# Block records by ScalarE, fewer weight transfers and a later subtraction in an attention and expert kernel

## The chip, the cores and the metric

The kernel runs on one core of a Trainium2 chip. A time is that of one execution on the device, in microseconds; lower is better. Before the change three timed runs gave 525.13, 525.26 and 527.0 us. The profiled execution, from which every duration below is read, took 523.72 us; its profile spans 521.8 of them.

## The reference

Sigmoid attention over 8 batches, 12 heads, 448 positions of width 64, and behind it a mixture of experts on the 3584 rows of 768 that it gives. A token goes to one expert of eight, and only where its skip score is above zero; all others keep the attention's output.

```python
attn = 1.0 / (1.0 + np.exp(-scores))
attn_out = np.matmul(attn, v)
...
do_compute = x @ w_skip > 0
e_idx = np.argmax(xc @ w_gate, axis=1)
gate_w = probs[np.arange(len(xc)), e_idx]
for e in range(E):
    h = np.maximum(xc[mask] @ w1[e], 0.0)
    y[mask] = gate_w[mask, None] * (h @ w2[e])
out[do_compute] = xc + y
```

The weights w1 are 768 x 1024 and w2 1024 x 768 for each expert, all in float32.

## The kernel before

The attention fills the first 280 us: a static list of steps, one for each batch and pair of heads. While it runs, each token's gate value and row number go as a record of 16 numbers into a list in device memory, `lst`, one stretch for each expert. At its end the kernel plans the rest on VectorE (lines 897 to 1086): how many blocks of tokens each expert gets, in which order, and at which row of `lst` each block begins. The two blocks of the first expert run before the loop, with their matmuls written out between the planning steps.

Then comes a loop (line 1565), one arm for each block, and each arm is one of four kinds. A **full** arm (`block(i, False)`) takes 128 tokens with weights that are split into a high and a low part (wh, wl), three matmuls for each product. A **split** arm (`block(i, True)`) does the same and also splits the next expert's raw weights: ScalarE casts raw to wh (`hi1`, `hi2`), VectorE subtracts to wl (`lo1`, `lo2`), and GpSimd subtracts the last two of w2. A **half** (64 tokens) or **few** arm (32) takes the rest of an expert straight from its raw weights, and behind its matmuls SyncE issues the weights of the next expert (`load_w1`, `load_w2`). In the profiled execution the order is split, half, full, half, full, few, full, few, full, few, split, few, full, few.

Inside an arm the order on each engine is written out by hand. For the prediction these steps matter. `look_ahead` and `entry` load registers from the small table `slots`. `take_rec` copies the loaded record `rn` into `recs[:, 2]`; `advance` shifts the records by one block at the arm's end. `fetch`, on GpSimd, reads row numbers from `rn`, gathers the tokens `xn` of the block after next from `out`, and then gathers the next record into `rn`; TensorE turns `xn` round in the next arm (`turn_x`, into pxt). `put`, on GpSimd, copies the row numbers `rid` to `rp[0]` and adds the block's output to `out` by an indirect store; its small operations named jk read a few numbers of the output and so test that it is there. `shift` moves the list of row numbers `rix` by one block. The block before the loop gets its two first records and tokens by GpSimd gathers (`gather_rec`, `gather`), and eight first weight transfers go out on SyncE and ScalarE.

## Time and profile before

| | before |
|---|---|
| median of three timed runs | 525.26 us |
| profiled execution | 523.72 us |
| its span | 521.8 us |
| TensorE busy | 506.6 us |
| VectorE busy | 298.0 us |
| ScalarE busy | 278.8 us |
| GpSimd busy | 266.6 us |

In the profile PE is TensorE and PEld its loading of weights, DVE is VectorE, ACT ScalarE, POOL GpSimd and SP SyncE; a q behind a name is the engine's instruction queue. A row of the timeline gives the start, the duration, the engine, the line of the program, the operation, the tile written and those read, and in brackets how long the engine had been idle and what ended that.

### The profile page before, as it was taken

Reading aid. Unit: us, or ns where it says so; the run is one execution under the profiler, and the core shown is the slowest. Engines: PE = TensorE matmul, PEld = TensorE weight load, DVE = VectorE, ACT = ScalarE, POOL = GpSimd, SP = SyncE. Lnnn points to the kernel's source line nnn. Section 1 sums busy time; section 2 is a strip of 40 time slices with the busy share of each in tenths; the row PEclk is TensorE's granted clock in tenths of the full one; section 3 lists DMA queues with packets and bytes.
Section 4 is the critical chain, followed back from the end, with each engine's and each line's share of the span. In section 5 each row is a group of like instructions: output and inputs, shape, how many; then the busy total and the mean of one; then the engine's idle time right before and its main releaser. Section 6 shows DMA issues by size and latency. Waiting matters only on the chain.

```text
span 521.8 us, 15390 instructions
## 1 busy us (share of the span) xinstructions
PE 506.6 (97%) x5033; PEld 341.5 (65%) x5034; DVE 298.0 (57%) x721; ACT 278.8 (53%) x481; POOL 266.6 (51%) x418
## 2 busy tenths in 40 slices
PE   8999999999999999999999999999999999999991
PEld 6875555545555446555455989948669797978790
DVE  4556856658668678587684952872223323249532
ACT  5776776767767667677674211942122323267221
POOL 4523553443557775766674332373333545456654
PEclk9999999999999999999999999999999999999996
DMA  8998887897989989999955017859393969696932
GB/s 210 214 248 187 174 178 160 171 179 174 202 187 239 234 193 206 206 217 219 197 117 119 11 42 241 336 169 360 98 355 139 329 234 346 237 348 214 361 121 47
DMA packets 140288, 107.21 MB, mean 205 GB/s; under 512 B 97099, under 2 KB 112731, under 8 KB 140240
## 3 DMA queue, kind: packets, MB, share of 16 engines
q1 hardware_dynamic: 133456, 96.09, 69.8%
q0 software_dynamic: 4576, 8.65, 6.9%
q10 hardware_dynamic: 2208, 1.83, 1.1%
q8 instruction: 30, 0.49, 0.4%
q14 instruction: 18, 0.15, 0.1%
HBM read 98.49 MB, written 17.56 MB: 222 GB/s over the span
## 4 chain that ended last, share of the span: by engine, by line
PE 95%; ACT 1%; DVE 1%; POOL 1%; issue 1%; DMA 1%; ACTq 0%; POOLq 0%; DVEq 0%
PE s L212 25%; PE pa L240 24%; PE py L544 11%; PE ph L516 11%; PE b_ph L516 3%; PE b_py L544 3%; PE py L1416 3%; PE ph L1416 3%; PE py L1485 2%; PE ph L1485 2%; PE pxt L492 2%; PE pl L280 2%; PE pht L530 1%; PE pg L297 1%; DMA kq_first<-in_q_dram 1%
## 5 line engine op out<-in xcount | busy, mean ns | idle before, releaser
L232 ACT ACTIVATE at<-s,bias 128x896 f32<-128x896 f32 (+1 forms) x191 | 173.8, 913 | 79.5 <-PE s L212 70.5
L212 PE MATMUL s<-x 64*64 64x448 f32 (+1 forms) x1528 | 170.2, 496 | 0.7 <-DVE x L194 0.7
L240 PE MATMUL pa<-at,v 64*64 64x448 f32 (+1 forms) x1536 | 168.5, 490 | 0.0
L176 POOL COPY kq<-kq 32x896 f32<-32x896 f32 (+1 forms) x96 | 87.7, 913 | 92.3 <-DMA kq<-in_q_dram 56.3
L212 PEld LDWEIGHTS s<-x 64*64 64x64 f32 x1528 | 83.9, 191 | 49.1 <-issue 25.2
L240 PEld LDWEIGHTS pa<-at,v 64*64 64x64 f32 x1536 | 65.6, 133 | 55.0 <-issue 45.7
L194 DVE STREAM_TRANSPOSE x<-kq 128x448 f32<-128x448 f32 x94 | 81.0, 936 | 4.4 <-PE pa L240 4.4
L250 DVE TENSOR_TENSOR xt<-xt,pa 128x448 f32<-128x448 f32 x48 | 29.8, 620 | 52.6 <-ACT xt L673 52.6
L414 POOL DMA_INDIRECT lst<-rec,idx x32 | 31.7, 990 | 17.8 <-DVE xt L250 5.7
L486 POOL TENSOR_TENSOR wl<-wr,wh 128x384 fp32r<-128x384 f32 (+1 forms) x28 | 31.2, 1124 | 12.8 <-DVE wh L485 8.3
L255 DVE STREAM_TRANSPOSE y<-xt 128x448 f32<-128x448 f32 x48 | 31.0, 645 | 5.8 <-DMA out_dram<-y 4.4
L574 POOL DMA_INDIRECT out_dram<-ys,rp x15 | 23.5, 1570 | 16.6 <-issue 8.4
L525 ACT ACTIVATE hs<-ph 128x512 f32<-128x512 f32 x14 | 8.4, 597 | 42.8 <-PE ph L516 34.8
L544 PE MATMUL py<-wh,hh 128*128 128x384 f32 x112 | 29.9, 348 | 0.0
L544 PE MATMUL py<-wh,hl 128*128 128x384 f32 x112 | 28.9, 339 | 0.5 <-DVE hl L536 0.5
L544 PE MATMUL py<-wl,hh 128*128 128x384 f32 x112 | 28.7, 337 | 0.0
L502 DVE TENSOR_TENSOR xl<-pxt,xh 128x384 fp32r<-128x384 f32 x30 | 15.3, 552 | 21.3 <-ACT xf L1097 20.8
L516 PE MATMUL ph<-wl,xh 128*128 128x512 f32 x84 | 26.6, 403 | 0.0
L536 DVE TENSOR_TENSOR hl<-pht,hh 128x512 fp32r<-128x512 f32 x14 | 9.7, 690 | 29.6 <-ACT hh L535 28.2
L673 ACT ACTIVATE xt<-pa 128x448 f32<-128x448 f32 x48 | 25.7, 535 | 0.8 <-PE pa L240 0.8
L516 PE MATMUL ph<-wh,xh 128*128 128x512 f32 x84 | 25.7, 403 | 0.0
L516 PE MATMUL ph<-wh,xl 128*128 128x512 f32 x84 | 24.5, 396 | 0.0
(279 smaller groups left out, 686.8 us busy)
## 6 DMA issues: line engine op xcount, KB each, us to landing
raw<-in_moe_w_dram SPq DMA_DIRECT2D x62, 768.0 KB
v<-in_v_dram SPq DMA_DIRECT2D x48, 256.0 KB
out_dram<-y SPq DMA_DIRECT2D x192, 56.0 KB
kq<-in_k_dram SPq DMA_DIRECT2D x46, 224.0 KB
kq<-in_q_dram SPq DMA_DIRECT2D x46, 224.0 KB
wr<-in_moe_w_dram SPq DMA_DIRECT2D x12, 256.0 KB
wr<-in_moe_w_dram SPq DMA_DIRECT2D x16, 192.0 KB
lst<-fill SPq DMA_DIRECT2D x4, 464.0 KB
```

What stands on the lines that cost most here:

```text
L176: nc.gpsimd.tensor_copy(a[BT:, :, :, :BT], a[:BT, :, :, BT:])
L194: nc.vector.transpose(xs[:, n].rearrange("p (r j) -> p j r", j=NJ), t.rearrange("p (j d) -> p j d", d=D)[:, :, :BT],)
L212: nc.tensor.matmul(sc[m * D : (m + 1) * D, j, : qs.stop - qs.start], xs[r, 0, first::NR7], xs[r, 1, qs], start=True, stop=True,)
L232: nc.scalar.activation(at[:, :, :n], sc[:, :, :n], AF.Sigmoid, bias=bias, scale=SCALE)
L240: nc.tensor.matmul(pa[j * D : (j + 1) * D, r, qs], vt[rs, j, r + c if c < 3 else 3 * (1 - r), :], at[rs, j, : qs.stop - qs.start], start=( ...
L250: nc.vector.tensor_tensor(x, x, pa[:, 1, :S], op=ALU.add)
L255: nc.vector.transpose(y, xts[b][:, hp, :])
L414: put = nc.gpsimd.indirect_dma_start(out=lst[:, :], out_offset=bass.IndirectOffsetOnAxis(ap=idx[:, c : c + 1], axis=0), in_=rec[:, c, :], ...
L486: nc.gpsimd.tensor_tensor(lo, r, hi, op=ALU.subtract)
L516: nc.tensor.matmul(ph[h], a[:, j * P : (j + 1) * P], w[j][h], start=(n == 0), stop=(n == len(t) - 1),)
L544: last = nc.tensor.matmul(half_y(py, o), a[h][:, js], w[j][:, o * H2 : (o + 1) * H2], start=(j == 0 and n == 0), stop=(j == NK2 - 1 and n ...
L1416: nc.tensor.matmul(dst[g * SM : (g + 1) * SM, :n], a, w, start=(j == 0), stop=(j == most - 1), tile_position=(0, g * SM),)
```

## The change

The table of row numbers for every lane goes, and with it the matmul that spread it and the VectorE operations that made it. The plan's table `slots` gets a fourth line, the row of `lst` at which a block's record begins. A record is then 128 rows in one piece: the first three come by plain transfers on SyncE, and in the loop one comes on ScalarE (`next_rec`) in place of the gather on GpSimd. `shift` goes. The cast of the row numbers moves from `advance` to `take_rec` of the next arm. In a split arm GpSimd's two subtractions go behind its store. The raw weights w1 come in three transfers in place of four, and the last two first transfers of w2 move from ScalarE's queue to SyncE's, ahead of the others.

```diff
     V.tensor_scalar(m_p, rho, af, f_p, op0=ALU.is_equal, op1=ALU.mult)
-    V.tensor_scalar(row, m_f, f_rf, None, op0=ALU.mult)
-    V.scalar_tensor_tensor(row, m_a, f_ra, row, op0=ALU.mult, op1=ALU.add)
-    V.scalar_tensor_tensor(row, m_p, f_rp, row, op0=ALU.mult, op1=ALU.add)
     gemm1(1, range(3), xh0, xl0, ph)
-    nc.tensor.matmul(ptab[:, :NS], ones_f, row, start=True, stop=True)
-    HAS, NXT, TYP = range(3)
-    for n, (j, m) in enumerate(((2, m_a), (7, m_p), (12, m_f))):
+    ROW, HAS, NXT, TYP = range(4)
+    for n, (j, m) in enumerate(((1, m_a), (6, m_p), (11, m_f))):
         nc.tensor.matmul(
-            ptab[:3, NS : 2 * NS], gt[:NS, j : j + 3], m, start=(n == 0), stop=(n == 2)
-        )
-    V.tensor_scalar(rix, ptab[:, :NS], slot_q, None, op0=ALU.add)
-    slots = const.tile([3, NS], I32, name="slots")
-    V.tensor_scalar(slots, ptab[:3, NS : 2 * NS], 0.25, None, op0=ALU.add)
+            ptab[:4, :NS], gt[:NS, j : j + 4], m, start=(n == 0), stop=(n == 2)
+        )
+    slots = const.tile([4, NS], I32, name="slots")
+    V.tensor_scalar(slots, ptab[:4, :NS], 0.25, None, op0=ALU.add)
     def entry(j, col, engines, most):
         return nc.values_load(slots[j : j + 1, col], engines=engines, min_val=0, max_val=most)
...
                 AF.Copy,
             )
-    def ready_x():
+    def ready_x(pieces=3):
         for h in range(2):
             hi_x(h, pxt[h], xh)
         for h in range(2):
-            whole_x(h, [slice(j, j + 1) for j in range(3)])
+            whole_x(h, [slice(j, j + 3 // pieces) for j in range(0, 3, 3 // pieces)])
         for h in range(2):
             lo_x(h, pxt[h], xh, xl)
-    def gather_rec(dst, idx):
-        nc.gpsimd.indirect_dma_start(
-            out=dst,
-            out_offset=None,
-            in_=lst[:, :],
-            in_offset=bass.IndirectOffsetOnAxis(ap=idx, axis=0),
-            bounds_check=NE * CAP - 1,
-            oob_is_err=False,
-        )
+    def load_rec(dst, col, engines=SP, queue=nc.sync):
+        row = entry(ROW, col, engines, NE * CAP - P)
+        queue.dma_start(dst, lst[ds(row, P), :])
     for j in range(2):
-        gather_rec(recs[:, j, :], rix[:, j + 2 : j + 3])
-    gather_rec(rn, rix[:, 4:5])
+        load_rec(recs[:, j, :], slice(j + 2, j + 3))
+    load_rec(rn, slice(4, 5))
     gemm1(1, range(3, 9), xh0, xl0, ph)
     turn0(0)
     nc.vector.tensor_copy(rid[:, 0:1], recs[:, 0, 1:2])
...
 
-    w1s = iter([(h, g) for h in range(2) for g in range(2)])
-    raw1g = {}
+    parts1 = ((0, 0, 3), (0, 3, NK1), (1, 0, NK1))
+    raw1g = []
     raw2g = []
     def some1(n):
         for _ in range(n):
-            h, g = next(w1s)
-            raw1g[h, g] = mo.tile([P, 3, H1], F32, name=f"raw1_{h}_{g}")
+            h, a, z = parts1[len(raw1g)]
+            raw1g.append(mo.tile([P, z - a, H1], F32, name=f"raw1_{h}_{a}"))
     def some2(n):
         for _ in range(n):
...
     def next_expert(col):
         return entry(NXT, col, SP, NE - 1), entry(HAS, col, SP, 1)
-    def load_w1(g, h, nx):
+    def load_w1(n, nx):
+        h, a, z = parts1[n]
         return nc.sync.dma_start(
-            raw1g[h, g],
-            w1[ds(nx[0], 1), g * 3 * P : (g + 1) * 3 * P, h * H1 : (h + 1) * H1].rearrange(
+            raw1g[n],
+            w1[ds(nx[0], 1), a * P : z * P, h * H1 : (h + 1) * H1].rearrange(
                 "o (i p) f -> p (o i) f", p=P
             ),
             cond=nx[1],
         )
-    def load_w2(g, nx, queue=nc.sync):
-        queue.dma_start(
+    def load_w2(g, nx):
+        nc.sync.dma_start(
             raw2g[g],
             w2[ds(nx[0], 1), g * 2 * P : (g + 1) * 2 * P, :].rearrange(
                 "o (i p) f -> p (o i) f", p=P
...
         nc.values_load(first_i[0:1, 0:1], engines=SP, min_val=0, max_val=1),
     )
-    nx_act = (
-        nc.values_load(first_i[0:1, 1:2], engines=[ET.Activation], min_val=0, max_val=NE - 1),
-        nc.values_load(first_i[0:1, 0:1], engines=[ET.Activation], min_val=0, max_val=1),
-    )
-    for n in range(4):
-        load = load_w1(n % 2, n // 2, nx)
+    for n in range(3):
+        load = load_w1(n, nx)
         if n == 1:
             tc.add_manual_dep(
                 load.ins,
...
             )
         if n == 0:
             look_ahead(slice(2, 3))
-    for g in range(4):
-        load_w2(g, nx if g < 2 else nx_act, nc.sync if g < 2 else nc.scalar)
+            for g in range(2, 4):
+                load_w2(g, nx)
+    for g in range(2):
+        load_w2(g, nx)
     def fetch():
         pool.tensor_tensor(xn[:, 0:1], xn[:, 0:1], zf, op=ALU.add)
-        pool.tensor_tensor(jk, rn[:, 0:2], rn[:, 0:2], op=ALU.add)
         pool.tensor_copy(ri, rn[:, 1:2])
-        pool.tensor_tensor(rn[:, 0:1], rn[:, 0:1], zf, op=ALU.add)
-        pool.tensor_tensor(rx, rix[:, 5:6], zero, op=ALU.add)
         pool.tensor_tensor(rp[1], ri, zero, op=ALU.add)
         pool.tensor_tensor(rq, rp[1], zero, op=ALU.add)
         got = gather(xn, rp[1])
         tc.declare_no_dep(got.ins, group="put", across_iterations=True, reason="a token is in one block only")
         tc.add_to_no_dep_group("got", got.ins)
-        gather_rec(rn, rx)
-    def shift(eng):
-        for to, src in ((riv, rix[:, 6:NS]), (rix[:, 5 : NS - 1], riv)):
-            if eng is pool:
-                eng.tensor_tensor(to, src, zero.to_broadcast([P, NS - 6]), op=ALU.add)
-            else:
-                eng.tensor_copy(to, src)
+    def next_rec(i):
+        load_rec(rn, ds(i + 5, 1), [ET.Activation], nc.scalar)
     def put(n, last=None):
 
...
             nc.vector.tensor_copy(sv[:, j * n : (j + 1) * n], recs[:, 1 + j * n : 1 + (j + 1) * n, 0:2])
         for j in range(pieces):
             nc.vector.tensor_copy(recs[:, j * n : (j + 1) * n, 0:2], sv[:, j * n : (j + 1) * n])
+    def take_rec():
+        nc.vector.tensor_copy(recs[:, 2, 0:2], rn[:, 0:2])
         nc.vector.tensor_copy(rid[:, 0:1], recs[:, 0, 1:2])
-    def take_rec():
-        nc.vector.tensor_copy(recs[:, 2, 0:2], rn[:, 0:2])
     def weigh_sum(y, p, gate):
         nc.vector.tensor_scalar(y, p, gate, None, op0=ALU.mult)
...
         if last:
             for h in range(2):
                 whole_x(h, (slice(0, 3),))
-            shift(dve)
         else:
-            ready_x()
+            ready_x(1)
+        next_rec(i)
         for j in range(1, NK2):
             gemm2(j, hh, hl, py)
         if last:
...
                 lo2(j)
             for j in range(NK2 - 2, NK2):
                 dve.tensor_copy(wh2[j], raw2[j])
-                pool.tensor_tensor(wl2[j], raw2[j], wh2[j], op=ALU.subtract)
             for h in range(2):
                 lo_x(h, pxt[h], xh, xl)
-        else:
-            shift(dve)
         for o in range(2):
             rows = ys if last else yt
             weigh_sum(rows[:, o * H2 : (o + 1) * H2], half_y(py, o), recs[:, 0, 0:1])
         put(P, last)
         advance(1 if last else 2)
         if last:
-            for j in range(2, NK2 - 2):
-                lo2(j)
+            for j in range(2, NK2):
+                lo2(j, dve if j < NK2 - 2 else pool)
     def few(i):
 
...
                 nc.vector.scalar_tensor_tensor(
                     yt[:SM, s], p, recs[:SM, 0, 0:1], yt[:SM, s], op0=ALU.mult, op1=ALU.add
                 )
+        next_rec(i)
         put(SM)
         advance()
 
```

On GpSimd, at the end of a split arm, these stand before the change, from the gather of the next record to the jump back. In the names, raw_3 holds the raw weights, wh_6 and wl_6 the high and low part of one slice of w2, rp_4354 the row numbers of the block.

```order
L1115 DMA rn<-lst,rx 128x16
L1396 TENSOR_TENSOR wl_6_130<-raw_3_4371,wh_6_122 128x768
L1396 REGISTER_ALU
L1396 TENSOR_TENSOR wl_7_131<-raw_3_4371,wh_7_123 128x768
L1308 TENSOR_TENSOR rp_4354<-rid,zero 128x1
L1309 REGISTER_ALU
L1309 TENSOR_TENSOR rs<-rp_4354,zero 128x1
L1314 REGISTER_ALU
L1314 TENSOR_TENSOR jk<-ys 128x2
L574 DMA out_dram<-ys,rp_4354 3584x768
L1560 UNCONDITIONAL_BRANCH
```

The same place on GpSimd with the change (the names' numbers differ by build):

```order
L561 DMA xn<-out_dram,rp_4370 128x768
L1280 REGISTER_ALU
L1280 TENSOR_TENSOR rp_4369<-rid,zero 128x1
L1281 REGISTER_ALU
L1281 TENSOR_TENSOR rs<-rp_4369,zero 128x1
L1286 REGISTER_ALU
L1286 TENSOR_TENSOR jk<-ys 128x2
L571 DMA out_dram<-ys,rp_4369 3584x768
L1224 REGISTER_ALU
L1224 TENSOR_TENSOR wl_6_127<-raw_3_4383,wh_6_119 128x768
L1224 REGISTER_ALU
L1224 TENSOR_TENSOR wl_7_128<-raw_3_4383,wh_7_120 128x768
```

The gather of the record is gone, and the two subtractions stand behind the store, the last work of the arm.

On VectorE, in a split arm before the change, from the first high-low difference of the hidden values (hl) on; the cast of rid stands at the arm's end, behind the copies that advance the records:

```order
L536 TENSOR_TENSOR hl_4352<-pht,hh_4349 128x512
L1343 COPY recs<-rn 128x2
L1234 REGISTER_ALU
L1234 TENSOR_TENSOR wl_3_0_110<-raw_0_1_4348,wh_3_0_98 128x512
...
L1336 COPY sv<-recs 128x4
L1338 REGISTER_ALU
L1338 COPY recs<-sv 128x2x2
L1339 ISA
L1339 CAST rid<-recs 128x1
L1240 REGISTER_ALU
L1240 TENSOR_TENSOR wl_2_126<-raw_1_4368,wh_2_118 128x768
```

The same places on VectorE with the change:

```order
L533 TENSOR_TENSOR hl_4367<-pht,hh_4364 128x512
L1314 COPY recs<-rn 128x2
L1315 REGISTER_ALU
L1315 CAST rid<-recs 128x1
L1216 REGISTER_ALU
L1216 TENSOR_TENSOR wl_3_0_107<-raw_0_3_4363,wh_3_0_95 128x512
...
L1308 COPY sv<-recs 128x4
L1310 REGISTER_ALU
L1310 COPY recs<-sv 128x2x2
L1224 REGISTER_ALU
L1224 TENSOR_TENSOR wl_2_123<-raw_1_4380,wh_2_115 128x768
```

The cast has moved from the arm's end to the middle of the next arm, behind hl and the copy of the record; in a few or half arm `take_rec` is the first work of VectorE.

On SyncE, ahead of the loop, from the first loads of `slots`; before the change:

```order
L1089 TENSOR_LOAD slots
L1089 ISA x2
L1213 ISA
L1213 DMA raw_0_0_4347<-in_moe_w_dram 128x3x512
L1213 ISA
L1213 DMA raw_0_1_4348<-in_moe_w_dram 128x3x512
```

With the change:

```order
L1079 TENSOR_LOAD slots
L1079 ISA x2
L1105 ISA
L1105 DMA recs<-lst 128x16
L1079 TENSOR_LOAD slots
L1079 ISA x2
...
L1195 DMA raw_0_0_4362<-in_moe_w_dram 128x3x512
L1204 ISA
L1204 DMA raw_2_4382<-in_moe_w_dram 128x2x768
L1204 ISA
L1204 DMA raw_3_4383<-in_moe_w_dram 128x2x768
L1195 ISA
```

Three record transfers with their register loads now stand ahead of the first weights, and the transfers of raw_2 and raw_3 ahead of the second weight transfer.

## Rows read from the trace of the kernel before

**Rows 1.** The page: busy time of each engine with its share of the span and its instructions, and the shares of the chain that ended last, by engine.

```profile
PE 506.6 (97%) x5033; PEld 341.5 (65%) x5034; DVE 298.0 (57%) x721; ACT 278.8 (53%) x481; POOL 266.6 (51%) x418
...
PE 95%; ACT 1%; DVE 1%; POOL 1%; issue 1%; DMA 1%; ACTq 0%; POOLq 0%; DVEq 0%
```

**Rows 2.** The waits of TensorE's matmuls from 280 us to the end, two of three (the third, 0.2 us, lies at 281 us): who waited for whom; total us, times, longest us.

```profile
PE py L1416 <- ACT xh L498: 0.8, 1, 0.8
PE py L544 <- DVE hl L536: 0.5, 1, 0.5
```

**Rows 3.** Stretches of whole arms: from and to, length, then the busy time of PE, PEld, DVE, ACT and POOL with their instructions, the granted clock as a share, the share of the DMA engines and GB/s. In this order the first split arm, the second split arm, a few arm behind a full one, the few arm behind the second split arm.

```profile
321.84:340.36 18.52, 18.52 (x101) 16.42 (x101) 12.64 (x22) 13.08 (x25) 5.63 (x10) 1.00 0.86 317
458.65:477.96 19.31, 18.82 (x102) 16.48 (x106) 13.29 (x30) 14.81 (x28) 10.92 (x19) 1.00 0.89 301
452.10:458.65 6.55, 6.55 (x137) 4.72 (x137) 2.55 (x10) 2.52 (x12) 3.88 (x11) 1.00 0.67 220
477.96:485.51 7.55, 6.79 (x138) 5.02 (x137) 7.33 (x13) 3.07 (x13) 6.27 (x8) 1.00 0.73 245
```

**Rows 4.** The chain that ended last, in order of time: start, us, what. The matmul that spreads the row numbers, and the turning of the tokens in the full arm behind the second split arm and its few arm.

```profile
307.43 0.41 PE ptab L1077 x2
...
494.55 0.65 PE pxt L492 x6
```

**Rows 5.** Timeline of VectorE from the end of the few arm into the second split arm.

```profile
464.70 0.15 DVE L1339 CAST rid<-recs 128x1 int32<-128x1 f32 x1 [3.58 <-POOL rp L1308]
466.85 1.90 DVE L1234 TENSOR_TENSOR wl<-raw,wh 128x512 fp32r<-128x512 f32 x3 [2.00 <-PE ph L516]
468.78 0.69 DVE L536 TENSOR_TENSOR hl<-pht,hh 128x512 fp32r<-128x512 f32 x1
```

**Rows 6.** Timelines of VectorE (the first row from the end of the first split arm, the others from the end of the second and the few arm behind it) and of GpSimd from the same end of the second split arm.

```profile
341.80 1.14 DVE L1346 TENSOR_SCALAR ys<-py,recs 128x384 f32<-128x384 f32 x2
...
479.58 1.13 DVE L1346 TENSOR_SCALAR ys<-py,recs 128x384 f32<-128x384 f32 x2
480.63 1.63 DVE L1336 COPY sv<-recs 128x4 f32<-128x4 f32 x1
...
482.80 3.56 DVE L1240 TENSOR_TENSOR wl<-raw,wh 128x768 fp32r<-128x768 f32 x4
...
478.61 3.61 POOL L1396 TENSOR_TENSOR wl<-raw,wh 128x768 fp32r<-128x768 f32 x2 [3.39 <-DVE wh L1395]
...
482.59 0.19 POOL L1314 TENSOR_TENSOR jk<-ys 128x2 f32<-128x2 f32 x1
483.33 1.92 POOL L574 DMA_INDIRECT out_dram<-ys,rp  x1 [0.55 <-issue]
...
488.07 1.08 POOL L564 DMA_INDIRECT xn<-out_dram,rp  x1 [0.74 <-PE ph L516]
```

**Rows 7.** Time from issue to landing of the token gathers in the loop (least, median, most of all 15), and of the one of 488.07 alone.

```profile
DMA to landing us min/median/max: 3.4/5.4/6.8
...
DMA to landing us min/median/max: 6.1/6.1/6.1
```

**Rows 8.** Timelines: GpSimd's fetch in a few arm behind a full one, first operation and gather, and then VectorE and GpSimd in the second split arm.

```profile
456.86 0.18 POOL L1286 TENSOR_TENSOR xn<-xn,zf 128x1 f32<-128x1 f32 x1 [0.19 <-PE py L1416]
...
458.76 1.08 POOL L564 DMA_INDIRECT xn<-out_dram,rp  x1 [0.75 <-PE py L1416]
...
469.45 3.69 DVE L1234 TENSOR_TENSOR wl<-raw,wh 128x512 fp32r<-128x512 f32 x6
...
470.14 0.64 POOL L1290 TENSOR_TENSOR rx<-rix,zero 128x1 int32<-128x1 int32 x1
470.75 0.65 POOL L1291 TENSOR_TENSOR rp<-ri,zero 128x1 int32<-128x1 int32 x1
```

**Rows 9.** Timelines of VectorE and GpSimd at the end of the program, in the last few arm.

```profile
511.41 1.26 DVE L1473 SCALAR_TENSOR_TENSOR yt<-py,recs,yt 32x384 f32<-32x384 f32 x2 [0.17 <-ACT yt L1471]
...
512.10 1.00 POOL L1115 DMA_INDIRECT rn<-lst,rx  x1 [0.30 <-issue]
...
514.15 0.18 POOL L1314 TENSOR_TENSOR jk<-yt 32x2 f32<-32x2 f32 x1
...
515.66 1.41 POOL L574 DMA_INDIRECT out_dram<-ys,rp  x1 [0.62 <-issue]
```

**Rows 10.** Ahead of the loop: VectorE's write of the table, SyncE's register loads from it (durations in ns, least, median, most; first and last start), GpSimd's first token gather, TensorE's turning of its rows.

```profile
308.50 0.20 DVE L1086 TENSOR_SCALAR slots<-ptab 3x64 int32<-3x64 f32 x1
...
L1089 SPq TENSOR_LOAD <-slots x3: 262/269/269, 308.7 to 309.9; - x3
...
312.82 1.00 POOL L564 DMA_INDIRECT xc<-out_dram,rid  x1 [0.30 <-issue]
...
317.87 0.82 PE L492 MATMUL pxt<-ident,xc 128*128 128x128 f32 x6
```

**Rows 11.** Time from issue to landing of the record gathers (least, median, most), a weight transfer issued on ScalarE's queue, and at the head of the second split arm ScalarE's first relu and the TensorE operation that waits for it.

```profile
DMA to landing us min/median/max: 2.3/4.2/6.1
...
319.12 0.39 ACTq L1222 DMA_DIRECT2D raw<-in_moe_w_dram  x1
...
463.17 0.60 ACT L525 ACTIVATE hs<-ph 128x512 f32<-128x512 f32 x1 [3.16 <-PE ph L516]
464.98 0.60 PE L530 MATMUL pht<-ident,hs 128*128 128x128 f32 x4
```

More of the change, by code (lines that the diff above doesn't have):

```diff
@@ L95 @@
     nc.gpsimd.iota(slot_i, pattern=[[1, 1]], base=0, channel_multiplier=1)
-    ones_f = const.tile([NS, P], F32, name="ones_f")
-    nc.vector.memset(ones_f, 1.0)
     lst = dram.tile([NE * CAP, REC], F32, name="lst")
@@ L105 @@
     rid = const.tile([P, 3], I32, name="rid")
-    rix = const.tile([P, NS], I32, name="rix")
     wh1 = [
@@ L897 @@
     grids = wk.tile([NS, 6 * NS], F32, tag="A", name="grids", bufs=5)
-    rho, m_f, m_a, m_p, row, rampn = (
+    rho, m_f, m_a, m_p, rampn, ramp_n = (
         grids[:, j * NS : (j + 1) * NS] for j in range(6)
     )
-    nc.gpsimd.iota(row.bitcast(I32), pattern=[[1, NS]], base=0, channel_multiplier=0)
+    nc.gpsimd.iota(ramp_n.bitcast(I32), pattern=[[1, NS]], base=0, channel_multiplier=0)
     V = nc.vector
@@ L1027 @@
     V.tensor_reduce(gt, d17, axis=AX.X, op=ALU.add)
-    f_a, f_ra, f_ha, f_na, _, f_p, f_rp, f_hp, f_np, _, _, _, f_hf, _, f_last, f_f, f_rf = (
+    f_a, f_ra, f_ha, f_na, _, f_p, f_rp, f_hp, f_np, _, _, f_r, f_hf, _, f_last, f_f, f_rf = (
         gt[:NS, j : j + 1] for j in range(17)
@@ L1036 @@
     V.memset(f_hf, 0.0)
+    V.tensor_copy(f_r, f_rf)
     V.tensor_scalar(f_last, f_last, 0.0, float(SPLIT), op0=ALU.is_gt, op1=ALU.mult)
@@ L1061 @@
     relu0(0, ph)
-    V.tensor_copy(rampn, row.bitcast(I32))
+    V.tensor_copy(rampn, ramp_n.bitcast(I32))
     beg = small("beg", 1)[:NS]
@@ L1190 @@
     rs = mo.tile([P, 1], I32, name="rs")
-    rx = mo.tile([P, 1], I32, name="rx")
     sv = mo.tile([P, 2, 2], F32, name="sv")
-    riv = mo.tile([P, NS - 6], I32, name="riv")
     jk = mo.tile([P, 2], F32, name="jk")
     yt = mo.tile([P, DM], F32, name="yt")
-    skip(4616 - DM)
-    some1(2)
+    skip(4688 - DM)
+    some1(1)
     some2(2)
@@ L1200 @@
     some2(2)
-    raw1 = [[raw1g[h, i // 3][:, i % 3, :] for h in range(2)] for i in range(NK1)]
+    raw1 = [[raw1g[i // 3][:, i % 3, :], raw1g[2][:, i, :]] for i in range(NK1)]
     raw2 = [raw2g[j // 2][:, j % 2, :] for j in range(NK2)]
@@ L1237, in hi2, with lo2 @@
         nc.scalar.activation(wh2[i], raw2[i], AF.Copy)
-    def lo2(i):
-        nc.vector.tensor_tensor(wl2[i], raw2[i], wh2[i], op=ALU.subtract)
     dve, pool = nc.vector, nc.gpsimd
+    def lo2(i, eng=dve):
+        eng.tensor_tensor(wl2[i], raw2[i], wh2[i], op=ALU.subtract)
     ET = mybir.EngineType
@@ L1338, in advance @@
             nc.vector.tensor_copy(recs[:, j * n : (j + 1) * n, 0:2], sv[:, j * n : (j + 1) * n])
-        nc.vector.tensor_copy(rid[:, 0:1], recs[:, 0, 1:2])
     def take_rec():
         nc.vector.tensor_copy(recs[:, 2, 0:2], rn[:, 0:2])
+        nc.vector.tensor_copy(rid[:, 0:1], recs[:, 0, 1:2])
     def weigh_sum(y, p, gate):
@@ L1433, in few @@
             nc.scalar.activation(hs[:, s], ph[c][:, :P], AF.Relu)
-        for h in range(2):
-            for g in range(2):
-                load_w1(g, h, nx)
+        for n in range(3):
+            load_w1(n, nx)
         nc.tensor.transpose(turned[0][:, :P], hs[:, parts[0]], ident)
@@ L1445, in few @@
         ready_x()
-        shift(dve)
         for n in range(4):
@@ L1500, in half @@
             nc.scalar.activation(hs[:, s], ph[0][:, s], AF.Relu)
-        for h in range(2):
-            for g in range(2):
-                load_w1(g, h, nx)
+        for n in range(3):
+            load_w1(n, nx)
         for h in range(2):
@@ L1515, in half @@
         ready_x()
-        shift(dve)
         ht8 = ht.rearrange("p (c h t) -> p c h t", c=4, h=2)
@@ L1537, in half @@
             weigh_sum(ys[:MD, s], py[1][o * MD : (o + 1) * MD, :H2], recs[:MD, 0, 0:1])
+        next_rec(i)
         put(MD)
```

2 lines of the change are left out of this document (removed).

## The prediction

> **What bounds the kernel now.** I read the page first. TensorE is busy for 97% of the span and the chain that ended last lies on it for 95% [rows 1], so a microsecond counts only where TensorE stands still, or before its first and behind its last matmul. Next the waits of TensorE from 280 us on: it waited for another engine twice only, 0.8 and 0.5 us [rows 2]. The stretches by arm say what these two cost, with the refilling of the pipeline: the first split arm took 18.52 us, the second 19.31; a usual few arm 6.55, the one behind the second split arm 7.55 [rows 3]. So 0.79 + 1.00 us can be had in the loop. The chain then shows the other two places: two passes of a matmul for the row numbers, 0.41 us [rows 4], and the tail, where GpSimd alone works [rows 9]. All other edits touch engines that wait for TensorE.
>
> **The change part by part.** The sum is made against the profiled execution, 523.72 us (span 521.8 and 1.9 around it); the median of the runs shown, 525.26, lies 1.54 above it, and a difference found here is taken over to it.
>
> Row-number table. The matmul with ones_f goes: -0.41 us, on TensorE's path [rows 4]. The remaining three matmuls get a fourth column and cost the same; three VectorE operations and a cast go beside other work.
>
> First records on SyncE. The table was ready at 308.50 + 0.20 us [rows 10], now some 0.4 earlier, 308.3. SyncE spaces register loads by 0.6 us [rows 10]; with an issue of 0.4 (that of a ScalarE transfer [rows 11]) the first record is under way at 309.3, the others at 310.3 and 311.3. How soon so small a transfer lands is not shown; the nearest rows are those of the gathered record, 2.3 to 6.1 us [rows 11], so it is there between 311.6 and 315.4. The token gather behind it was issued at 312.82 and TensorE wants its rows at 317.87, now 317.46 [rows 10]; landings of token gathers run from 3.4 to 6.8 us [rows 7]. From end to end this is between no cost and 315.4 + 6.8 - 317.46 = 4.7 us. I take no cost: the stage loads almost nothing else, so both landings should lie at their lower ends, 311.6 + 3.4 = 315.0, and two GpSimd gathers no longer stand ahead of the token gather. SyncE's first weight load moves some 2 us later, behind three transfers and six register loads; it is read only in the first arm, some 15 us on, and the two loads that leave ScalarE's queue go ahead of the wait for the last matmul of the block before. TensorE didn't wait in that arm [rows 2], so earlier weights give nothing.
>
> Row cast an arm later. At the end of a few arm VectorE's cast stood 3.58 us for GpSimd's copy of the row numbers, until 464.70; the next subtraction began 2.00 us after the cast, at 466.85 [rows 5], and the hl for which TensorE waited came at 468.78. In the first split arm the same subtraction began 5.7 us after the arm's start; here it would be about 464.3, and hl follows its own ScalarE input, near 466.3, well ahead of 469. The 0.79 us goes. In its new place the cast stands behind hl, and what is queued behind it (the next subtractions) isn't wanted for several microseconds.
>
> GpSimd subtracts behind its store. In the second split arm GpSimd's two subtractions ran from 478.61 for 3.61 us. VectorE's copy of a few numbers took 1.63 us and ended with them; the first matmul of the few arm's second product waited over the same stretch [rows 6]. With the subtractions gone from there this wait goes too: -1.00 us. But they go somewhere: between this store and the fetch of the next tokens, and there beside VectorE's own four. With -0.41, -0.79 and -1.00 the split arm ends at 476.76 and the next full arm starts at 483.31; TensorE turns the new tokens 494.55 - 485.51 = 9.04 us into it [rows 3, 4], so they are wanted at 492.35. VectorE ends its output 341.80 + 1.14 - 340.36 = 2.58 us after the split arm's end [rows 3, 6]: 479.34. The store starts 0.74 behind the test of that output and takes 1.92 [rows 6]: it ends near 482.05. VectorE's four subtractions (3.56 us [rows 6]) run from about 479.8 to 483.3. Do the two engines' subtractions hold each other up? The trace has no pair of large ones side by side. The nearest: GpSimd operations that take 0.18 us alone took 0.64 and 0.65 between VectorE's subtractions, which went on at one per 0.6 us [rows 8]; each ended with one of them. And VectorE's copy was held for as long as a GpSimd subtraction ran [rows 6]. So I take them one after another: 482.05 + 1.25 left of VectorE's + 3.61 = 486.9. Bounds: 485.66 with no hindrance, 489 if each waits for all of the other (482.05 + 3.56 + 3.61 = 489.2). The fetch then needs 1.90 us to its gather [rows 8], less three dropped operations of 0.14 each: 1.48, so 488.4; that gather landed 6.1 us after issue, under the weight loads of the few arm [rows 7]. Tokens at 494.5, 2.15 us late; the transposes come at 494.5 where they came at 494.55. The whole gain on TensorE up to there is given back, at that one place.
>
> [...]
>
> Records by ScalarE. GpSimd loses the record gather and three small operations in each arm. ScalarE gets a register load and an issue, about 0.6 + 0.4 us per arm. Behind them stand, in a block arm, the casts of later weights, and after a few arm the next arm's relu, before which ScalarE idled 3.16 us [rows 11]. The new landing lies between 2.3 and 6.1 us as above; the record is used some 7 us into the block arm behind a few arm, and some 4 us after its issue at the head of a few or half arm, where only xl stands behind it and is wanted later still. Cost: none. Were the cover gone, the relu may slip by another 464.98 - 463.17 - 0.60 = 1.2 us before TensorE waits [rows 11].
>
> Tail. VectorE's last output is ready at 511.41 + 1.26 = 512.67; GpSimd came to the second half's test at 514.15 only, since the record gather of 512.10 and small operations stood in front [rows 9]. Without them the test can start near 512.8, and the last store with it: -1.35 us, the end of the program behind it. Fewer, longer transfers of the weights, and fewer xf copies in full arms, are on engines that wait: nothing.
>
> Sum: -0.05 - 1.35 = -1.4 us, 522.3 by the profile, 523.9 against the median.
>
> **The rivals.** First: the subtractions pass each other unhindered. For it: no such pair is seen. Then GpSimd ends at 485.66, the gather is issued at 487.14 and lands at 493.24; 1.3 us more stay: 522.6. Second: the tokens are not late at all, since a gather lands at the lower end, 3.4 us. Against it: every gather beside a few arm's weight loads lay near 6. All 2.2 us stay: 521.7. Third: nothing comes of it; the last store's landing, or a little wait of the kind in rows 2 at another place, sets the end again: 525.2. Fourth, on the other side: ScalarE's new transfer holds its queue until the record's source is read by GpSimd or the old record is done, at the end of few arms. It decides from a hold of 3.16 + 1.2 = 4.4 us. With a landing of 4.2 added to the 1.0 it is 0.8 us late, with 6.1 it is 2.7, in each of four few arms followed by a block: 3.2 to 10.8 us, so 527.1 to 534.7. Against it: the old record and its readers are done microseconds earlier in a usual few arm.
>
> **How the numbers follow.** Forecast 0.50 (own range 523.2 to 524.7), first rival 0.20, second 0.10, third 0.12, fourth 0.08. About 0.5%, 2.6 us, is what a measurement of this kernel can tell from no change: below 522.6 is faster, above 527.9 slower. Faster: the second rival, half of the first and a little of the forecast, 0.23. Slower: most of the fourth, 0.07. Same: 0.70. The range goes from 521.7, where the second rival lies, to 526.2, the third with half a microsecond and part of the late first records.
>
> **What would show it.** Right: the second split arm near 18.5 us and the few arm behind it near 6.55; in the full arm behind, a wait of TensorE's transposes for the gathered tokens of 1 to 2.5 us that was not there before; GpSimd's two subtractions ending near 487 by the old clock; the last store some 3.6 us after TensorE's last matmul, not 5.0. Wrong: no wait at these transposes, a wait of TensorE for a relu, or one for the first tokens before the loop.

## The result, and the profile after

The changed kernel takes 529.18 us against 525.26 (medians of 15 runs each): the ratio is 1.0068, its 95% interval 1.0049 to 1.0087. One run of each kernel, 871.74 and 589.97 us, lies far off the others and is left out of the ratio. The changed kernel is slower, by 3.9 us where 1.4 less was forecast. Its profiled execution took 527.02 us, its span is 525.3; a second profile of the same kernel (e1 below) has a span of 528.0.

The table gives the lengths of the stretches of TensorE, us, each read from the starts of the first matmuls in the timelines. ([rows 3] counts the first split arm from the end of the matmul ahead of it, so it has 18.52 us there for the 18.61 here.) The last column is e16, the fastest version found.

| stretch | before | changed | changed, second profile | e16 |
|---|---|---|---|---|
| attention | 280.37 | 281.96 | 281.58 | 281.57 |
| to the loop's first matmul | 41.31 | 42.62 | 43.12 | 40.91 |
| first split arm | 18.61 | 19.11 | 20.13 | 18.45 |
| half arm behind it | 12.22 | 12.37 | 12.33 | 12.29 |
| full arms, first four | 18.54 to 18.56 | 18.38 to 18.42 | 18.38 to 18.42 | 18.38 to 18.41 |
| second split arm | 19.31 | 18.56 | 18.56 | 18.41 |
| few arm behind it | 7.55 | 6.61 | 6.62 | 6.63 |
| full arm behind that | 18.55 | 21.19 | 22.80 | 18.40 |
| behind the last matmul | 11.16 | 10.73 | 10.75 | 10.85 |
| span | 521.8 | 525.3 | 528.0 | 519.7 |

The attention isn't touched; other profiles of the kernel before with small edits (e7, e8, e12, e17) have it at 281.06 to 282.64, so I take its 1.6 us for chance. The other rows make 1.9 us in the first profile and 5.0 in the second.

The waits of TensorE in the changed kernel from 300 us on (who for whom; total us, times, longest). Neither wait of [rows 2] is there, and four new ones are:

```profile
PE ph L513 <- DVE rid L1315: 2.5, 1, 2.5
PE ph L513 <- issue: 1.5, 1, 1.5
PE ph L1453 <- ACT wh L1219: 0.7, 1, 0.7
PE py L1453 <- ACT ht L1481: 0.2, 1, 0.2
```

The stretches that answer to [rows 3], columns as there: loop entry, first split arm, second split arm, few arm and full arm behind it.

```profile
322.90:324.58 1.68, 0.14 (x2) 0.03 (x1) 1.14 (x2) 0.00 (x0) 0.08 (x1) 1.00 0.91 296
324.58:343.69 19.11, 18.42 (x99) 16.53 (x99) 11.75 (x21) 13.71 (x26) 3.97 (x8) 1.00 0.69 250
461.54:480.10 18.56, 18.48 (x101) 16.55 (x99) 13.14 (x26) 14.86 (x28) 10.17 (x16) 1.00 0.92 314
480.10:486.71 6.61, 6.61 (x136) 4.59 (x136) 6.54 (x10) 3.02 (x13) 3.38 (x4) 1.00 0.58 220
486.71:507.90 21.19, 18.70 (x102) 16.45 (x98) 9.22 (x18) 4.76 (x10) 10.84 (x22) 1.00 0.77 262
```

Both stalls that were to go are gone (18.56 and 6.61), and the full arm loses more than they gave. Timelines of VectorE, GpSimd and TensorE there, which answer to [rows 6]:

```profile
482.98 7.76 DVE L1224 TENSOR_TENSOR wl<-raw,wh 128x768 fp32r<-128x768 f32 x4
490.66 0.16 DVE L1314 COPY recs<-rn 128x2 f32<-128x2 f32 x1
490.73 0.14 DVE L1315 CAST rid<-recs 128x1 int32<-128x1 f32 x1
...
483.52 1.89 POOL L571 DMA_INDIRECT out_dram<-ys,rp  x1 [0.58 <-PE pxt L489]
484.89 4.15 POOL L1224 TENSOR_TENSOR wl<-raw,wh 128x768 fp32r<-128x768 f32 x2
...
490.87 1.66 PE L513 MATMUL ph<-wl,xh 128*128 128x512 f32 x6 [2.49 <-DVE rid L1315]
```

VectorE's four subtractions took 7.76 us where they took 3.56, GpSimd's two 4.15 for 3.61. One row of the line's instructions (durations in ns, least, median, most; first and last start) says how:

```profile
L1224 DVE TENSOR_TENSOR wl<-raw,wh x4: 944/955/5149, 483.0 to 489.8; 128x768 fp32r<-128x768 f32 x4
```

Three took 0.95 us as ever, and one 5.15. It began just before GpSimd's pair and ended behind it, 4.20 us longer than the others: as long as GpSimd ran. VectorE's next two steps, the record and the cast, came after that, and TensorE's full arm waits for them.

The entry of the loop shows the second loss, the wait of 1.54 us at 324.58, put down to `issue`, that is, to nothing that the profile ties to it. It is TensorE's branch into the first arm, in the profile on its weight-load queue (ns, least, median, most of 14), first before, then changed; the longest of each is the first of the 14:

```profile
L1554 PEldq COMPARE_BRANCH  x14: 74/83/487, 320.4 to 502.1; - x14
```

```profile
L1521 PEldq COMPARE_BRANCH  x14: 74/83/2527, 321.6 to 506.1; - x14
```

And so the tail, GpSimd's last steps, answers to [rows 9]:

```profile
510.97 1.61 POOL L571 DMA_INDIRECT out_dram<-ys,rp  x1 [0.58 <-issue]
...
516.65 0.18 POOL L1280 TENSOR_TENSOR rp<-rid,zero 128x1 int32<-128x1 int32 x1 [1.11 <-DVE yt L1440]
...
519.15 1.38 POOL L571 DMA_INDIRECT out_dram<-ys,rp  x1 [0.60 <-issue]
```

The last store starts 4.57 us behind the last matmul (514.58); before it was 5.05, forecast 3.6.

### The profile page after: what moved, and what is told of

Read it like the earlier page. It is cut to its first block, busy times and chain, and to the rows that moved or that the text cites. A ratio compares the mean times of both kernels' runs of the same rounds, so it can differ in the third digit from the quotient of the medians.

```text
span 525.3 us, 15265 instructions
## 1 busy us (share of the span) xinstructions
PE 505.9 (96%) x5031; PEld 338.5 (64%) x5032; DVE 298.5 (57%) x688; ACT 277.1 (53%) x461; POOL 246.1 (47%) x359
## 4 chain that ended last, share of the span: by engine, by line
PE 91%; DMA 2%; issue 2%; DVE 2%; POOL 1%; ACT 1%; ACTq 0%; DVEq 0%; POOLq 0%; SPq 0%
PE s L209 25%; PE pa L237 23%; PE ph L513 11%; PE py L541 11%; PE b_ph L513 3%; PE b_py L541 3%; PE ph L1453 2%; PE py L1453 2%; PE ph L1385 2%; PE pl L277 2%; PE pxt L489 2%; PE py L1385 2%; PE pht L527 1%; DMA out_dram<-ys,rp 1%; PE pg L294 1%
## 5 line engine op out<-in xcount | busy, mean ns | idle before, releaser
L209 PE MATMUL s<-x 64*64 64x448 f32 (+1 forms) x1528 | 164.6, 496 | 1.8 <-DVE sel L404 1.1
L237 PE MATMUL pa<-at,v 64*64 64x448 f32 (+1 forms) x1536 | 162.7, 489 | 0.0
L209 PEld LDWEIGHTS s<-x 64*64 64x64 f32 x1528 | 79.2, 191 | 53.8 <-issue 30.2
L237 PEld LDWEIGHTS pa<-at,v 64*64 64x64 f32 x1536 | 61.3, 133 | 56.1 <-issue 50.0
```

The costliest lines, as they stand in the source:

```text
L209: nc.tensor.matmul(sc[m * D : (m + 1) * D, j, : qs.stop - qs.start], xs[r, 0, first::NR7], xs[r, 1, qs], start=True, stop=True,)
L237: nc.tensor.matmul(pa[j * D : (j + 1) * D, r, qs], vt[rs, j, r + c if c < 3 else 3 * (1 - r), :], at[rs, j, : qs.stop - qs.start], start=( ...
```

## The experiments

Theories: **lock** (VectorE stands while GpSimd subtracts), **code** (the early weights delay what TensorE needs to enter the loop), against the forecast's own reading and chance. "Before" stands for runs of the kernel before on the same chip; all ratios are to it. Lengths of arms are read as in the table.

**e1, the changed kernel again.**

> The changed kernel as it is, for a second profile of it: its first profiled execution took 527.02 us, 2.2 below its median, so what makes the rest is not in that trace. Lock theory (VectorE stands while GpSimd subtracts): VectorE's four lo2 subtractions of the second split arm take 7.5 to 8 us again and TensorE waits 2 to 3 us in the full arm behind. Code theory (TensorE's first branch into the loop fetches behind the weight transfers that now go ahead of the wait): the branch takes over 2 us again, and varies more than the first. Rival (chance waits in the attention and elsewhere): neither wait is there again, and TensorE's waits lie at other places.

528.2 us, ratio 1.0064 (1.0042 to 1.0086). VectorE's four took 7.77 us, the wait in the full arm is 2.50, the branch took 3.05 us and the wait at the entry 2.06. New is what follows both waits. Stretches, columns as in [rows 3]:

```profile
324.70:330.00 5.30, 5.29 (x16) 4.22 (x17) 0.00 (x0) 0.00 (x0) 0.42 (x1) 0.68 0.96 329
330.00:340.00 10.00, 10.00 (x57) 8.98 (x56) 7.95 (x15) 8.88 (x18) 3.83 (x7) 1.00 0.65 256
487.00:492.00 5.00, 2.50 (x19) 1.23 (x11) 5.00 (x5) 0.88 (x2) 4.92 (x5) 1.00 1.04 320
492.00:497.00 5.00, 5.00 (x15) 3.96 (x16) 2.51 (x8) 0.56 (x2) 3.40 (x11) 0.66 1.04 377
```

Behind the waits of 2.06 and 2.50 us the granted clock is 0.68 and 0.66 of full speed, as the mean of 5.3 and 5.0 us. The full arm takes 22.80 us where it took 21.19 in the first profile, whose wait of 2.49 was followed by 1.00. Against the 18.40 of e16 the same wait cost 4.4 us or 2.8; no row here shows what decides. This makes most of the difference of the two profiles. It is likely also why the runs of this kernel spread over 5 us: in the first fifteen the mean granted clock is 0.995 in the fastest run (526.29 us) and 0.986 in the slowest that the ratio counts (531.84).

**e2, GpSimd's two back ahead of its store; e3, no early weights; e4, both.**

```diff
-            for j in range(2, NK2):
-                lo2(j, dve if j < NK2 - 2 else pool)
+            for j in range(2, NK2 - 2):   # e2, e4; lo2(j, pool) behind the casts, as before
+                lo2(j)
```

```diff
-            for g in range(2, 4):         # e3, e4
-                load_w2(g, nx)
-    for g in range(2):
+    for g in range(4):
         load_w2(g, nx)
```

> The changed kernel with GpSimd's two subtractions back ahead of its store. Lock theory: VectorE's four take 3.6 us again and the wait of 2.49 us in the full arm goes; the few arm ahead of it pays 0.8 to 1.0 us as before the change. Net 1.5 us faster than the changed kernel, about 527.5 us. Rival (the wait of 2.49 us is only the cast's new place, not the subtractions): the wait stays, and the time rises to 530.

> The changed kernel with the two early transfers of w2 back behind the wait for the last matmul of the block before the loop, all on SyncE. Code theory: TensorE's first branch takes 0.5 us in place of 2.53, the first split arm starts without the wait of 1.54 us; the last w1 transfer lands no later, so the half arm's wait of 0.69 stays or goes: 1.5 to 2.4 us faster than the changed kernel, 526.8 to 527.7. Rival (the branch is slow by chance or by the kernel's new layout): no gain, 529; second rival: all weights now come later, ScalarE's casts in the first split arm wait for them, and the half arm loses what the branch gained.

> Both undone, the subtractions' place and the early transfers. If lock and code theory hold and add up: 3.0 to 3.9 us faster than the changed kernel, 525.3 to 526.2, the time of the kernel before or a little under it by the removed matmul (0.41) and the cast (0.87). If the rest of the change (records by ScalarE, first records on SyncE) costs something too, it stays above 526.5.

e2: 525.71 us, ratio 1.0016 (1.0000 to 1.0031). e3: 526.58, 1.0051 (1.0026 to 1.0076). e4: 524.94, 1.0002 (0.9992 to 1.0013). In e2 VectorE's four take 3.56 us and the full arm 18.39, and the few arm ahead takes 7.85; the early weights are still there and the branch takes 2.91 us. The time came 1.8 us lower than the 527.5 expected. In e3 the branch takes 0.49 us and the arm is entered without a wait, while the full arm still takes 21.17. The median of e3 alone does not show its gain, since its interval and that of e1 overlap; the trace shows it. Within this noise the gains add up: 2.5 and 1.6 us under e1, 3.3 both together, which is the whole loss. But in e4 a branch of 1.73 us and a wait of 0.74 are left, the half arm waits 0.84 us, and the few arm takes 7.82 us where it took 7.55 before the change; this eats what the other parts gave.

**e5, no subtraction on GpSimd; e6, also no weight transfer at all ahead of the last matmul.** Both on e3:

```diff
-                lo2(j, dve if j < NK2 - 2 else pool)
+                lo2(j)
     # e6 alone
-        if n == 1:
+        if n == 0:
             tc.add_manual_dep(
```

> The changed kernel with all weights behind the wait (as in e3) and all six subtractions of w2 on VectorE, none on GpSimd. Lock theory: nothing holds VectorE; at 0.89 us each its six end 5.4 us after they begin, 1.8 us later than the four do alone and 2.4 us earlier than they did in the changed kernel, so of the wait of 2.50 us 0.1 remains, and the few arm pays nothing either: 2.4 us under e3, about 524.2, and 0.7 under e4. Rival (VectorE's own amount of work is the bound, not GpSimd): six take 5.4 + the 4.2 that they were longer, and the wait in the full arm grows.

> e5 with the first w1 transfer too behind the wait for the last matmul, so that no weights are on the way when TensorE branches into the loop. Code theory: the branch took 0.49 us in e3 and 1.73 in e4, both with one early transfer; with none it takes 0.5 us or less, each time, 0.2 to 0.7 us faster on the median. Rival: all weights come later, ScalarE's casts in the first split arm wait for them by 1 to 2 us, and the half arm starts late: 1 us slower than e5.

524.93 us, 1.0004 (0.9989 to 1.0019); 526.65, 1.0034 (1.0021 to 1.0047). VectorE's line in e5, as above:

```profile
L1224 DVE TENSOR_TENSOR wl<-raw,wh x6: 949/950/959, 481.7 to 486.0; 128x768 fp32r<-128x768 f32 x6
```

Six in 5.30 us with none held up, and the full arm takes 18.40: the amount of work on VectorE was not the bound. The time stayed above the 524.2 expected, since the few arm took 7.45 us and the first split arm 19.84. In e6 the branch takes 0.49 us as in e5, so it gains nothing, and the casts wait for the late weights (split arm 21.61): its rival was right.

**e7, e8: the kernel before with one of the two parts alone.** e7 has the early weights, e8 GpSimd's two subtractions behind its store.

```diff
     # e7, in the kernel before
-    for g in range(4):
-        load_w2(g, nx if g < 2 else nx_act, nc.sync if g < 2 else nc.scalar)
+            for g in range(2, 4):         # under n == 0, ahead of the wait
+                load_w2(g, nx)
+    for g in range(2):
+        load_w2(g, nx)
```

> The kernel before with one part of the change alone: two transfers of w2 on SyncE ahead of the wait for the last matmul (in place of ScalarE's queue). Code theory: TensorE's first branch into the loop takes 2.5 to 3 us in place of 0.49, the first split arm starts 1.5 to 2.1 us late, 1.5 to 2.5 us slower than before, 526.5 to 527.5. Rival (the branch is slow only with the changed kernel's code): 525.0, no difference.

> The kernel before with the other part alone: GpSimd's two subtractions behind its store. Lock theory: VectorE's four take 7.7 us in place of 3.56; the wait in the few arm (1.0) goes, and one of about 2.5 us comes in the full arm behind it, now and then with a dip of the clock behind: 1.5 to 2.5 us slower, 526.5 to 527.5. My forecast's reading (VectorE goes on, GpSimd yields, only the tokens are late): no more than 0.5 us either way.

e7: 527.31 us, 1.0051 (1.0029 to 1.0073). e8: 528.63, 1.0086 (1.0057 to 1.0115), of six runs. e8 alone is as slow as the whole change: VectorE's four take 7.78 us, TensorE waits 3.16 in the full arm, and the clock is 0.72 behind it. The wait and the stretch, columns as in [rows 3]:

```profile
PE ph L516 <- DVE recs L1343: 3.2, 1, 3.2
```

```profile
490.00:496.00 6.00, 6.00 (x20) 4.73 (x21) 2.81 (x11) 0.60 (x1) 4.46 (x13) 0.72 1.04 379
```

In this code the cast isn't moved, and the wait ends with the next operation of VectorE's queue, the copy of the record: it is the queue that is late, not one result. e7 is slower by the amount expected, but at another place; TensorE's waits from 300 us on:

```profile
PE pxt L492 <- DMA xc<-out_dram,rid: 2.0, 1, 2.0
PE py L1418 <- ACT xh L498: 0.8, 1, 0.8
PE py L544 <- DVE hl L536: 0.3, 1, 0.3
```

Its branch took 0.40 us; the first tokens came 2.0 us late instead: their gather landed 7.2 us after its issue, 3.9 before. So it is not the branch as such that the early weights delay: here the tokens came late beside them, by 2.0 us, and in the changed kernel the branch ended late, after 2.53 us.

The DMA packets of the traces show one thing more there. Some of them are of the kind "instruction"; in the changed kernel one of them falls within the slow branch, 321.59 to 324.12 us (queue, kind: packets, MB, share of 16 engines):

```profile
q8 instruction: 1, 0.02, 2.4%
```

It began at 321.75 and took 0.97 us. In the five profiles whose first branch took over 0.49 us (the changed kernel, e1, e2, e4, e15) the branch ended 1.38 to 1.41 us behind the end of such a packet; in the other fifteen the packet had ended 1.70 us or more ahead of the branch's end. Counted from the end of the attention the packet began at 36.3 to 37.9 us without the early transfers of w2 and at 39.8 to 40.3 with them, in e7 at 39.1. So a long branch, 2.53 us beside 0.08 for a usual one, ended at one distance behind such a packet, and the packet came later with the early weights. That the branch waited for code that this packet brought is my reading of these times; no row ties the two. The exception is e4, 39.0 without the early transfers: that one stays open.

**e9 to e11, w1 in four transfers; e15, the same with the records on GpSimd's queue.** e9 is e5 with `parts1` in four, e10 has one of VectorE's subtractions ahead of its casts too, e11 besides a tile of its own for the rows of a few arm's store.

```diff
-    parts1 = ((0, 0, 3), (0, 3, NK1), (1, 0, NK1))
+    parts1 = ((0, 0, 3), (0, 3, NK1), (1, 0, 3), (1, 3, NK1))
     # e10, e11, and later e14, e16 to e18; the last loop then runs over range(3, NK2)
-            for j in range(2):
+            for j in range(3):
                 lo2(j)
     # e15, and later e13, e14, e16
-        load_rec(rn, ds(i + 5, 1), [ET.Activation], nc.scalar)
+        load_rec(rn, ds(i + 5, 1), [ET.Pool], nc.gpsimd)
```

> e5 with w1 again in four transfers of 768 KB. Transfer theory: the second half of w1 came in one piece of 1.5 MB, all of which ScalarE's cast had to wait for (0.65 to 1.1 us idle for raw in the changed kernel, e3 and e5, 0.17 before); with two pieces that wait is 0.2 us again, ScalarE is earlier, and the half arm's wait of 0.7 to 1.3 us goes: the first split arm takes 18.6 us in place of 19.84, 0.8 to 1.2 us faster, 523.7 to 524.1. Rival (the half arm waits for the record that ScalarE loads, as one row in e3 says, or for casts that come late because all loads start late): the wait stays, 524.9.

> e9 with one of VectorE's six late subtractions in the 0.9 us that it idles ahead of its casts of w2. If the 0.9 us that the few arm still loses in e5 (7.45 against 6.55) is a wait for VectorE's last work of the split arm, as the wait ending with its second subtraction says: the few arm takes 6.6 to 7.0, 0.5 to 0.9 us faster than e9. Rival (it is something else in the few arm, the weights' transfers for example): 7.45 stays.

> e10 with a tile of its own for the row numbers of a few arm's store, so that the last store need not wait until the store before it has landed (5.5 us after its issue in the changed kernel, when GpSimd had been idle for 1.1 us). If that wait is what was left of the 1.35 us that I forecast for the tail: 0.5 to 1.0 us from the end, tail 10.0 to 10.3 in place of 10.8. Rival (the output's last part is ready no earlier): 0.3 or less.

> e9 (w1 in four transfers) with the records on GpSimd's queue. [...] Rival (four transfers, or nine of any kind, are slow in themselves): 540 or more stays.

546.15, 545.64 and 545.58 us: 20 us slower, which no theory had. The arms that e10 and e11 are about can still be read. The few arm behind the second split arm took 6.63 us in e10 and 7.60 in e9, as expected. The tail of e11 took 10.77 us where 10.0 to 10.3 was expected (10.48 in e10), and in its chain the copy of the row numbers still follows the landing of the store before, 5.64 us after the issue: the shared tile was not what it waits for. VectorE's waits in e9 and one of them in the timeline:

```profile
DVE recs L1312 <- ACTq L1558: 42.0, 6, 8.1
```

```profile
427.88 0.17 DVE L1312 COPY recs<-rn 128x2 f32<-128x2 f32 x1 [8.11 <-ACTq L1558]
```

The copy of the record stands 8.11 us in a full arm, and the row names only an instruction of ScalarE's queue as what came last. Another row of the same waits ends one of the copy's with a landing of weights; the changed kernel has none such from 300 us on:

```profile
DVE recs L1312 <- DMA raw<-in_moe_w_dram: 2.0, 1, 2.0
```

That the copy also stands for weights in the six waits of 42.0 us is my reading, which no row shows.

e15 takes 525.87 us (1.0006, 0.9985 to 1.0028): with the records on GpSimd's queue the 20 us are gone, with w1 still in four pieces. I had expected 523.5 to 524.5. So, with the records by ScalarE, w1 has to stay in three transfers here.

**e13, e14, e16, e18: the half arm's wait.** e13 is e5 with the records on GpSimd, e14 has e10's early subtraction too. e16 is e14, e18 the same with ScalarE's records, both with this:

```diff
-            ready_x(1)
+            ready_x()
```

> e5 with the loop's records loaded by plain transfers on GpSimd's queue in place of ScalarE's. [...]

> e13 with one of the six late subtractions earlier on VectorE, as in e10, where the few arm behind took 6.63 us in place of 7.59. If the gains add up: another 0.6 to 0.9 us, 522.8 to 523.4, faster than both kernels by 0.3 to 0.5%. Rival (the tail or another wait takes it back): 523.8 or more.

> e14 with the copies xf of a full arm again in six pieces. Count theory (the half arm's first matmul waits for a count of ScalarE's operations; with four fewer in a full arm the count that it needs is reached in a split arm only by the third of the last four casts): the wait of 1.77 us goes, the first split arm takes 18.6 us in place of 20.36; the full arms may return from 18.40 to 18.56 us if the copies are what made them faster. 0.8 to 1.8 us faster than e14, less up to 0.8. Rival (casts that are late because the weights are): the wait stays at 2.57 us after the casts' begin.

> e16 with the records on ScalarE's queue as in the changed kernel. Count theory alone: as e16, first split arm 18.6. Record theory beside it (the half arm's first matmul waits for the record's landing too, 6.3 to 7.2 us after its issue): the first split arm 19.2 to 19.8.

e13: 525.6 us, 0.9993 (0.9979 to 1.0007), and the wait of the half arm stayed, 0.96 us. I had expected it to go, 523.6 to 524.1 us: that the record's landing holds the half arm fell for this wait. e14: 525.04, 0.9980 (0.9964 to 0.9996), above the 522.8 to 523.4 expected, which was counted from the 523.6 to 524.1 of e13; the few arm took 6.61 us as hoped, the half arm waited 1.77. In the changed kernel, e5, e13 and e14 the half arm's first matmul began 2.57 or 2.58 us behind the begin of ScalarE's last four casts, here e13:

```profile
341.58 3.05 ACT L1219 ACTIVATE wh<-raw 128x768 fp32r<-128x768 f32 x4
...
344.15 1.17 PE L1451 MATMUL ph<-raw,xf 128*64 128x512 f32 x4 [0.96 <-ACT wh L1219]
```

and in e16 1.50 us behind it, with no wait:

```profile
339.43 3.23 ACT L1219 ACTIVATE wh<-raw 128x768 fp32r<-128x768 f32 x4
...
340.93 2.37 PE L1451 MATMUL ph<-raw,xf 128*64 128x512 f32 x10
```

The data of that matmul are the same in both. The edit only gives ScalarE four more operations in a full arm, and the wait in the half arm, 1.77 us in e14, is gone. That the matmul waits for a count of ScalarE's operations, common to all four kinds of arm, which was reached late in a split arm, is my reading; the rows show the two starts, 2.57 and 1.50 us behind the begin of the casts. e16 takes 523.09 us, 0.9969 (0.9954 to 0.9983): faster than both kernels. e18 takes 523.6, 0.9973 (0.9960 to 0.9985), no other time than e16 by the medians. In its profile the first split arm took 19.87 us and the half arm waited 0.6 us for the record's landing, so the record is a second limit there.

**e12, the kernel before with the cast alone; e17, also all late subtractions on VectorE, one of them early.**

```diff
     # e12, e17, in the kernel before
-        nc.vector.tensor_copy(rid[:, 0:1], recs[:, 0, 1:2])
 
     def take_rec():
 
         nc.vector.tensor_copy(recs[:, 2, 0:2], rn[:, 0:2])
+        nc.vector.tensor_copy(rid[:, 0:1], recs[:, 0, 1:2])
     # e17
-                pool.tensor_tensor(wl2[j], raw2[j], wh2[j], op=ALU.subtract)
...
-            for j in range(2, NK2 - 2):
+            for j in range(3, NK2):
                 lo2(j)
```

> The kernel before with the cast of the row numbers moved to the next arm, and nothing else. By the forecast's step: the second split arm takes 18.5 to 18.6 in place of 19.31, 0.7 us faster than before, 524.3; the few arm's 7.55 stays. Rival: the cast in its new place delays what stands behind it, and the gain comes back in the few or the full arm: 525.0.

> The kernel before with the cast moved (e12) and all six late subtractions on VectorE, one of them earlier, none on GpSimd. If the gains add up on the code before: second split arm 18.5 (19.31), few arm behind it 6.6 (7.55), no wait elsewhere: 1.6 us faster than before, 523.4 to 523.9. Rival (the full arm then waits for VectorE, which also has two copies of row numbers there in this code): 524.5 or more.

525.05 us, 0.9994 (0.9980 to 1.0007): the second split arm takes 18.51 us as forecast, but 0.8 us can't be told in the medians. e17 takes 523.32, 0.9972 (0.9960 to 0.9985), with 18.54 and 6.63 in the two arms: two edits on the code before are worth as much as the whole change mended.

## Why the prediction was wrong

- **Row-number table:** right. Where the loop is entered without a wait (e3, e5, e16) the stretch ahead of it takes 40.91 to 40.94 us for 41.31.
- **First records on SyncE:** no cost, right; the first tokens were there in time in the changed kernel. But "earlier weights give nothing" looked at what weights give and not at what they stand in front of. They cost a wait of 1.5 to 2.1 us at the entry, and in e1, with the granted clock of 0.68 behind it, 3.9 us (the stretch to the loop and the first split arm against e16). The first of them also moved 3.1 us later, counted from the end of the attention, and not some 2.
- **Row cast:** right, 0.75 us in the second split arm.
- **GpSimd subtracts behind its store:** the few arm's 0.94 us came as forecast. The step that failed is "482.05 + 1.25 left of VectorE's + 3.61": it lets VectorE finish and GpSimd yield. Measured, GpSimd's pair took 4.15 us and VectorE stood, 4.2 us in the middle of one subtraction, so the four ended at 490.7 in place of 486.5, and the full arm lost 2.6 us in the first profile (18.55 to 21.19) and 4.2 in the second. The forecast had the row for it: VectorE's copy of a few numbers that took 1.63 us, until GpSimd's pair ended [rows 6], is VectorE standing behind a large GpSimd operation. I gave the turn to VectorE by the short GpSimd operations of [rows 8] instead. And I followed only GpSimd's chain (the tokens), not what stands behind VectorE's subtractions on its own queue: the record, the cast, xl, and the full arm. The wait at the tokens' transposes didn't show, since TensorE stood earlier. The token gather itself was issued 5.3 us into the full arm, 5.1 in the forecast, but that is luck: GpSimd's pair ended 2.3 us into it and not 3.6, and then its next two small operations took 1.42 and 2.16 us beside VectorE's last two subtractions.
- **Whose turn it was:** VectorE's subtraction of 0.95 us became one of 5.15. Which of the two engines came first the trace can't settle: by its starts VectorE's held subtraction was first, 484.72 against 484.89 for GpSimd's, but the subtraction before it ended at 484.80 only, and GpSimd's times are rough in the profile. VectorE's ended at 489.87, behind both of GpSimd's, whose second ended at 489.04.
- **Records by ScalarE, longer transfers, fewer copies:** "on engines that wait: nothing" was wrong for the copies: 0.7 us at the half arm in the first profile, and 1.8 in e14, which e16 took away. The fourth rival didn't come: ScalarE's relu was never waited for.
- **Tail:** -1.35 forecast, -0.43 measured, -0.31 in e16. The removed gather was not alone: the copy of the row numbers that opens `put` began 2.1 us behind the last matmul, 2.5 before. GpSimd had been idle for 1.11 us then. By the chain it waited for the store of 510.97 to land, 5.53 us after its issue; the row's bracket names VectorE's output, which ended just before it too. A tile of its own (e11) didn't help, so what holds it is open.
- **The slower side:** I gave it 0.07 and saw it only in ScalarE's queue, where nothing came. What came was in my own reckoning, as one step on who yields.

## What to carry to other kernels

When work of two engines comes to lie side by side, as GpSimd's two subtractions beside VectorE's here, where one of 0.95 us became 5.15, the rows must say which of them stands, and then the queue of that one is to be followed, not only that of the engine whose work moved. A transfer brought forward off the critical path is to be weighed by what comes next to it as well: in e7 the first tokens landed 7.2 us after their issue and not 3.9, and in the changed kernel TensorE's first branch took 2.53 us and not 0.49. And a stall of TensorE cost more than its length in two runs: in e1 and e8 the granted clock was 0.66 and 0.72 over the 5 and 6 us behind waits of 2.50 and 3.16 us.

## What the runs showed that was not expected

- The same wait of 2.5 us was followed by the full clock, 1.00, in one execution (the changed kernel's first profile) and by 0.66 of it for 5 us in another (e1).
- Nine transfers in an arm in place of eight cost 20 us (e9, 546.15 us; 525.35 for the kernel before), with no more bytes.
- Four operations fewer on ScalarE in one kind of arm delayed TensorE in another kind (e14 against e16, 1.8 us).
- Full arms without a wait take 18.4 us in the kernels made from the changed one (e9 to e11 apart) and 18.55 in those made from the one before, with the same matmuls. The copies are not the cause (e16 has six and 18.40); it was not found.
